# A gated sum of windowed attention and a long convolution: spectrum and products in two halves of 40 channels a group, and a new order of all tasks

## The chip, the core and the metric

The kernel runs on one core of one Trainium2 chip. The time is the device time of one launch in microseconds (us). The core's engines each run their own queue of instructions in order: TensorE (PE, matmuls and their weight loads PEld), VectorE (DVE), ScalarE (ACT), GpSimd (POOL) and SyncE (SP, which here only starts transfers).

## The reference, cut to what matters

Everything is computed for 2048 positions of 640 channels in bfloat16. `a` is attention of 32 heads over 8 earlier positions with a step of 2; `b` is a convolution of every channel with a kernel K that is itself computed from 192 complex states per channel; the two are mixed by a gate.

```python
g = _sigmoid((x * gate_w).sum(-1, keepdims=True))
a = _A_ref(x, A_wqkv, A_wo)                  # q, k, v; 8 taps; softmax; times v; times wo
P = jnp.exp(logdA[:, :, None] * l[None, None, :])
K = jnp.einsum("dn,dnl,dn->dl", Cc, P, dB).real
Kf = rfft2(pad(K)); Uf = rfft2(pad(x.T))     # length 4096
b = irfft2(Uf * Kf)[..., :L].T + x * Dskip
return g * a + (1 - g) * b
```

## The kernel before, in words

The program is a list of named tasks (`pl.add(name, engines, function, ...)`). A table of numbers, `SEQ`, sets the one order in which all 1331 tasks are written down (a letter behind a number picks the engine where there is a choice: A for ScalarE, D for VectorE; S and G pick the queue of SyncE or GpSimd for a transfer). Each engine then runs its own tasks in that order. Short-lived buffers are rings: `acq` takes a slot, `rel` gives it back; `SLOTS` has their sizes, such as two two-bank accumulators `ar` and two one-bank accumulators `tb` in PSUM.

The tasks that the change and the prediction speak of:

- **Start.** `ldx` (four loads of x), `ldt` (three of wqkv) and the parameter loads; `turn`/`tev` transpose x by TensorE and copy the result out (10 pairs, tile 128x1024, into `bufA`); `lset` blanks two tables `L` on GpSimd (three MEMSETs each).
- **Attention.** `late`/`lev` project q, k, v (accumulator `tb`); for each of eight blocks of 256 positions VectorE multiplies (`prod`, L336), TensorE sums (`lg`), the softmax follows, VectorE weighs the values (`pv`, L405), TensorE gathers (`gat`), `oT`, `wo`, `ga`, and `gaS` stores the block.
- **K by chunks.** Ten chunks (0 to 9) of 64 channels in three parts: `arg` on TensorE, `act` (sine and exponential, L778, L780) on ScalarE, `pq` on VectorE (three TENSOR_TENSOR, L797 to L799; `pq92` is the last part of the last chunk), `kmm` on TensorE, `fin`. Five ring slots let `act` run ahead of `pq`. After every five chunks `move`/`kev` lay the result out in `KE`.
- **Spectrum of K.** For each of 32 steps (16 pairs of frequencies, real and imaginary), `wl` loads 160 KB of weights, `ks` runs 20 matmuls (L917) over `KE`, and `ske` moves the 128x640 result into `sk`, on VectorE with the lag-0 term `KD` added (L926) for the real part, on VectorE or ScalarE for the imaginary one.
- **Spectrum of x.** `rows` loads; `fu`/`fue` (20 pairs) is the first stage into `Bu`; `fp`/`fe` (L1063) the second into `su`; the products `ta`, `tc`, `Y` (L1082 to L1088) multiply it with `sk` on VectorE.
- **Back.** `inv`/`cp` (20 pairs, L1112) into `C`; `yp` the last stage; `st`, `tt`, `mx` mix with `gaF`; `out` stores. SyncE starts the loads of the constants `psi` and of `gaF` (`gaf`) before that.

Before, all 32 `ks` steps come after the last chunk, since each needs the `KE` of all ten; all 20 `fu` must be done before the first `fp`; the first `inv` waits for the last products. An evacuation is one instruction:

```python
def evict(nc, en, o, i):
    if en == "A": nc.scalar.activation(o, i, ACT.Identity)
    else:         nc.vector.tensor_copy(o, i)
```

## Time and profile before

| | |
|---|---|
| time, 3 runs | 345.36 us median (344.45 to 347.49) |
| profiled execution | 345.49 us, of which the span of the core 343.7 us |
| PE | 295.3 us busy, 86%, 4630 matmuls |
| DVE | 309.3 us, 90%, 409 instructions |
| ACT | 279.3 us, 81%, 398 instructions |
| POOL | 38.2 us, 11% |
| DMA | 47.05 MB, 137 GB/s mean |
| granted TensorE clock | 0.963 mean |

A share is a mean over stages with different limits, so the stretches are looked at apart. A matmul's duration holds its way through the pipeline, so its rate is read from how far starts lie apart (in the chain of waits), not from its mean duration. "Idle before" names what an engine waited for last.

### The profile page before, as it was taken

The page shows a single profiled execution, that of the slowest core. Times are in us where ns is not written, and L with a number is a line of the kernel's source. Part 1 is how long each engine was busy: PE and PEld are TensorE (multiplying, and loading weights), DVE is VectorE, ACT ScalarE, POOL GpSimd, SP SyncE. Part 2 cuts the span into 40 slices and gives each one's busy share as a digit, 9 for nine tenths or more (in the row PEclk, how much of TensorE's full clock was granted, in tenths as well). Part 3 has the DMA queues.
Part 4 walks back from the last instruction along what each step waited for, and adds up shares of the span by engine and source line. Part 5 has one row for each costly group of instructions (what it writes and reads, how often), then busy time and mean ns, then how long its engine had stood idle before and what let it go on. Part 6 is the DMA issues. An engine that isn't in the chain of part 4 may idle for free.

```text
span 343.7 us, 10819 instructions
## 1 busy us (share of the span) xinstructions
PE 295.3 (86%) x4630; PEld 191.1 (56%) x4630; DVE 309.3 (90%) x409; ACT 279.3 (81%) x398; POOL 38.2 (11%) x61
## 2 busy tenths in 40 slices
PE   0479999999789999999999798898999999996850
PEld 0345545544344445555545354466797799976740
DVE  3898999999997999999999999979876999999890
ACT  1698999767997999999999989998566766567781
POOL 8245200064100000000000000000000000000052
PEclk9999999999958999999999989999999999998995
DMA  7994508978573116499747369822232289970046
GB/s 255 392 319 67 123 12 230 237 180 234 151 152 74 24 37 150 117 126 114 122 69 157 85 111 141 138 55 61 79 96 63 78 246 257 214 194 4 2 123 187
DMA packets 79354, 47.05 MB, mean 137 GB/s; under 512 B 49818, under 2 KB 75290, under 8 KB 79050
## 3 DMA queue, kind: packets, MB, share of 16 engines
q1 hardware_dynamic: 76298, 37.94, 50.5%
q0 software_dynamic: 2336, 7.73, 7.0%
q8 instruction: 36, 0.59, 0.8%
q10 hardware_dynamic: 672, 0.70, 0.6%
q14 instruction: 12, 0.10, 0.1%
HBM read 31.84 MB, written 14.51 MB: 135 GB/s over the span
## 4 chain that ended last, share of the span: by engine, by line
PE 52%; ACT 36%; issue 3%; DVE 3%; DMA 3%; POOL 1%; ACTq 0%; POOLq 0%; DVEq 0%
PE tb L278 13%; ACT big L778 11%; ACT big L780 8%; PE kp L917 6%; PE ar L917 6%; PE ar L764 5%; PE kps L815 4%; PE tb L411 3%; PE tb L428 3%; DMA uga<-in_A_x_dram 3%; PE ar L1063 3%; ACT bufA L1161 2%; PE ar L1031 2%; ACT C L459 2%; ACT L780 2%
## 5 line engine op out<-in xcount | busy, mean ns | idle before, releaser
L278 PE MATMUL tb<-bufA 128*128 128x512 bf16 x300 | 73.6, 388 | 1.2 <-ACT bufA L459 0.8
L778 ACT ACTIVATE big<-ar 128x720 bf16<-128x720 int16 (+1 forms) x90 | 68.2, 834 | 3.5 <-PE ar L764 2.7
L764 PE MATMUL ar<-Rarg,L 64*128 64x208 bf16 (+4 forms) x600 | 50.5, 255 | 13.1 <-ACT big L778 6.7
L278 PEld LDWEIGHTS <-bufA 128*128 128x128 bf16 x300 | 33.0, 120 | 31.8 <-issue 9.6
L780 ACT ACTIVATE big<-ar 128x832 bf16<-128x832 f32 x60 | 48.2, 887 | 0.6 <-PE ar L764 0.5
L405 DVE TENSOR_TENSOR pv<-vc,asb 128x4096 bf16<-128x4096 bf16 (+1 forms) x24 | 46.0, 1926 | 0.6 <-DMA asb<-aS 0.6
L764 PEld LDWEIGHTS <-L 64*128 64x128 bf16 x600 | 21.6, 95 | 43.4 <-issue 38.4
L1181 POOL DMA_DIRECT2D out_dram<-bufA x12 | 6.8, 571 | 240.7 <-DVE bufA L1164 240.5
L459 ACT ACTIVATE bufA<-ar 128x1024 bf16<-128x1024 f32 x25 | 25.4, 1030 | 8.1 <-PE ar L1031 6.8
L459 ACT ACTIVATE tbx<-ar 128x640 bf16<-128x640 f32 x31 | 21.6, 703 | 12.2 <-PE ar L1063 9.0
L815 PEld LDWEIGHTS <-tbx 64*64 64x64 bf16 (+1 forms) x1280 | 24.1, 113 | 7.5 <-issue 5.1
L815 PE MATMUL kps<-tbx 64*64 64x40 bf16 (+1 forms) x1280 | 27.9, 188 | 0.2 <-ACT E L459 0.2
L428 PE MATMUL tb<-wo_sb,oT 128*128 128x320 bf16 x160 | 26.4, 300 | 0.2 <-ACT ga L437 0.2
L336 DVE TENSOR_TENSOR prod<-uga 128x2048 bf16<-128x2048 bf16 x20 | 24.0, 1219 | 0.9 <-PE lg L342 0.8
L799 DVE TENSOR_TENSOR tbx<-big 128x1280 bf16<-128x1280 bf16 x30 | 24.5, 816 | 0.0
L336 DVE TENSOR_TENSOR prod<-qk 128x2048 bf16<-128x2048 bf16 x20 | 23.9, 1218 | 0.0
L459 ACT ACTIVATE uga<-tb 128x512 bf16<-128x512 f32 x28 | 16.6, 598 | 7.5 <-PE tb L278 7.3
L411 PE MATMUL tb<-pv,ind 128*64 128x512 bf16 (+1 forms) x192 | 22.6, 357 | 0.1
L797 DVE TENSOR_TENSOR tbx<-big 128x1024 bf16<-128x1024 bf16 x30 | 20.5, 683 | 2.1 <-ACT big L778 2.1
L798 DVE TENSOR_TENSOR tbx<-big 128x1024 bf16<-128x1024 bf16 x30 | 20.5, 682 | 0.0
L183 PE MATMUL ar<-ident,uga 128*128 128x128 bf16 x80 | 7.5, 255 | 14.5 <-DMA uga<-in_A_x_dram 13.4
L428 PEld LDWEIGHTS <-oT 128*128 128x128 bf16 x160 | 13.7, 97 | 8.8 <-issue 2.3
(162 smaller groups left out, 543.1 us busy)
## 6 DMA issues: line engine op xcount, KB each, us to landing
vc<-vS SPq DMA_DIRECT2D x16, 327.5 KB, 5.6
Sprm<-pc SPq DMA_DIRECT2D x12, 240.0 KB, 3.9
L<-Sprm SPq DMA_DIRECT2D x80, 36.0 KB, 2.7
xS<-bufA POOLq DMA_DIRECT2D x2, 1280.0 KB, 6.7
gaS<-ga SPq DMA_DIRECT2D x16, 160.0 KB, 2.4
uga<-xS SPq DMA_DIRECT2D x8, 320.0 KB, 6.5
uga<-gaS SPq DMA_DIRECT2D x8, 320.0 KB, 13.9
W<-c_spec SPq DMA_DIRECT2D x14, 160.0 KB, 3.0
```

The source lines that it names most:

```text
L278: nc.tensor.matmul(ppf[:], self.wq[:, which, kt, e:D:5], self.xT[:, c0 // 1024, kt, c0 % 1024:c0 % 1024 + SC], start=(kt == 0), stop=(kt = ...
L336: nc.vector.tensor_tensor(b[e][:], self.part(ch, 0)[:, e, o:o + C].unsqueeze(1).to_broadcast([128, W, C]), win(self.part(ch, 1)[:, e, :], ...
L405: nc.vector.tensor_tensor(b["pv", e][:, 0:2 * n], taps, aw, ALU.mult)
L411: nc.tensor.matmul(b["op", e][64 * a:64 * a + 64, 0:n, :], self.twin, b["pv", e][:, a:2 * n:2, w, :], start=(w == 0), stop=(w == HV - 1), ...
L428: nc.tensor.matmul(apf[:, :320], b["oT"][:, e, i * 128:(i + 1) * 128], wo_sb[:, e, hf * 320:(hf + 1) * 320], start=(e == 0), stop=(e == 4))
L459: nc.scalar.activation(o, i, ACT.Identity)
L764: nc.tensor.matmul(ar[:, g2, wd * (j - j0):wd * (k - j0)], L[rows, sb, gp, l0:l0 + 128], R[rows, c0:c0 + wd * (k - j)], start=True, stop=T ...
L778: nc.scalar.activation(dst, ar[:].bitcast(I16)[:, :, 0:2 * n:2].rearrange("p g (j n) -> p g j n", n=wd), ACT.Sin, scale=SCL)
L780: nc.scalar.activation(dst, ar[:, :, 0:n].rearrange("p g (j n) -> p g j n", n=wd), ACT.Exp)
L799: nc.vector.tensor_tensor(qq[:, :, :, :], trg[:, :, KI:].rearrange("p a (v m) -> p a v m", v=2), exq[:, :, KI:].unsqueeze(2).to_broadcast( ...
L815: nc.tensor.matmul(kps[64 * w:64 * w + 64, 2 * NM * ql:2 * NM * ql + 2 * NM], pt[rows, v, k:k + 2, :].rearrange("p a n -> p (a n)"), qq[ro ...
L917: nc.tensor.matmul(kp[64 * c:64 * c + 64, fl, 0:320], w["t"][:, fl, m, :], self.KE[:, m, c].rearrange("p g x -> p (g x)"), start=(m == 0), ...
```

## The change

The 80 channels of each of eight groups are taken in two halves of 40 (p = 0 and 1; half 0 is chunks 0 to 4). What needed all ten chunks now needs five: `ks` has 64 steps of 20 matmuls with 160 columns instead of 32 steps with 320, and every `wl` load is made for either half (64 loads). `ske` moves 128x320. `Bu` and `sk` have a half each in `bufA` and in `big`, `rows` loads by halves, `fp` of a half needs ten `fu`; one `fp` holds four frequencies of 160 columns. `ta` and `tc` are one instruction over both parts instead of two; a `Y` is two. Half 0 of `inv` uses the accumulators `ar`, half 1 `cy`, and `gaf` also waits for half 0's last products. `ks` of half 0 uses `tb`, that of half 1 `ar` and two `kp`. The `SEQ` table is new throughout (1447 tasks).

```diff
 SEQ = """
-12A 10S 13S 24 0G 11A 25 28 16S 21 29 38 22 23 26 2G 1G 7G 3G 5G 6G 99 4S 14S ...
+0G 11S 13S 12A 25 23 16G 99 7S 101S 14A 10A 6A 24 22 28 38 29 3G 4G 102 103D ...
-    SLOTS = {... "kp": 1, ... "W": 6, "su": 2}
+    SLOTS = {... "kp": 2, ... "W": 5, "W2": 3, "su": 2, "sv": 2}
...
-        for k in range(32):
+        for z in range(64):
+            p, k = divmod(z, 32)
             i, ro = divmod(k, 2)
+            tag = "W2" if p and k % 8 > 4 else "W"
...
-                            nc.tensor.matmul(kp[64 * c:64 * c + 64, fl, 0:320], w["t"][:, fl, m, :], self.KE[:, m, c].rearrange("p g x -> p (g x)"),
-                                             start=(m == 0), stop=(m == M5 - 1), ...)
+                            nc.tensor.matmul(kp[64 * c:64 * c + 64, 160 * fl:160 * fl + 160], w["t"][:, fl, m, :], self.KE[p][:, m, c].rearrange("p g x -> p (g x)"),
+                                             start=(m == 0 and fl == 0), stop=(m == M5 - 1), ...)
...
-            m = pl.add(f"ks{ro}x{i}", "P", spec, deps=[ld] + self.kevs + (ends if ro else []), ...)
+            m = pl.add(f"ks{p}{ro}x{i}", "P", spec, deps=[ld] + self.kevs[0:2 * p + 2] + (ends if p else []), ...)
...
-        self.Bu = self.bufA[:].rearrange("p (c e f q g) -> p c e f q g", c=NCH, e=2, f=32, q=8)
-        self.sk = big[:].rearrange("p (r x f) -> p r x f", r=2, f=32)
+        mem = self.bufA, big
+        self.Bu = [m[:, 0:10240].rearrange("p (c e f q g) -> p c e f q g", c=NHF, e=2, f=32, q=8) for m in mem]
+        self.sk = [m[:, 10240:].rearrange("p (r x f) -> p r x f", r=2, f=32) for m in mem]
...
                 if k == 0:
-                    for r in range(2):
-                        nc.vector.tensor_tensor(t[r], u[0], kk[r], ALU.mult)
+                    nc.vector.tensor_tensor(t, u[:, 0].unsqueeze(1).to_broadcast(one), kk, ALU.mult)
                 elif k == 1:
-                    nc.vector.tensor_tensor(u[0], u[1], kk[1], ALU.mult)
-                    nc.vector.tensor_tensor(u[1], u[1], kk[0], ALU.mult)
+                    nc.vector.tensor_tensor(u, u[:, 1].unsqueeze(1).to_broadcast(one), kk[:, ::-1], ALU.mult)
                 else:
-                    nc.vector.tensor_tensor(kk[0], t[0], u[0], ALU.subtract)
-                    nc.vector.tensor_tensor(kk[1], t[1], u[1], ALU.add)
+                    nc.vector.tensor_tensor(kk[:, 0], t[:, 0], u[:, 0], ALU.subtract)
+                    nc.vector.tensor_tensor(kk[:, 1], t[:, 1], u[:, 1], ALU.add)
...
-            np_ = 4 if fb == 7 else 1
+            np_ = 2 if p and fb == 7 else 1
...
-                prev = pl.add(f"inv{cb}{ro}", "P", inv, deps=[self.muls[fb, 0] for fb in range(7)] + [self.muls[7, cb // 5]], ...)
+                prev = pl.add(f"inv{cb}{ro}", "P", inv, deps=[self.muls[p, fb, 0] for fb in range(8 - p)] + ([self.muls[1, 7, cl // 5]] if p else []), ...)
...
-            gas.append(pl.add(f"gaf{k}", "S", gaf, deps=[self.lastfu] + gaS, after=gas[-1:]))
+            gas.append(pl.add(f"gaf{k}", "S", gaf, deps=[self.lastfu, self.muls[0, 7, 0]] + gaS, after=gas[-1:]))
```

Three places show how the new table moves instructions. Lines of the changed kernel are a few higher than those of the kernel before (L699 is L703 there, L165 is L169).

**The start.** On GpSimd, behind the first small load, the kernel before has this (`in_A_wqkv` is one `ldt`, `in_A_x` three `ldx`, `MEMSET L` one `lset`):

```order
L249 DMA ind<-c_ind 128x96
L166 DMA bufA<-in_A_wqkv_dram 128x5x640
L165 DMA uga<-in_A_x_dram 128x2560 x3
L699 MEMSET L 128x1536
L701 MEMSET L 2x1536 x2
```

The changed kernel has this on GpSimd:

```order
L247 DMA ident<-c_ident 128x128
L555 DMA ldt<-in_B_log_dt_dram 128x5
L703 MEMSET L 128x1536
L705 MEMSET L 2x1536 x2
L169 DMA uga<-in_A_x_dram 128x2560 x3
```

The three loads of x stand behind the three MEMSETs now, and the wqkv load has gone to SyncE. On VectorE the kernel before starts with eighteen parameter instructions and has no copy of a transpose; the changed one, from its third parameter instruction on, has (`CAST bufA<-ar` is a `tev`):

```order
L581 TENSOR_TENSOR wi<-cre,bim 128x960
L581 TENSOR_TENSOR wr<-cre,bre 128x960
L581 TENSOR_TENSOR wi<-wi,t_123 128x960
L465 CAST bufA<-ar 128x1024
L581 TENSOR_TENSOR wr<-wr,t_122 128x960
L465 CAST bufA<-ar 128x1024
```

So VectorE's parameter work waits for x there, and two of the first five `tev` are its own.

**The last chunk on VectorE.** Before, from `pq90` on, one after the other (`tbx<-big` is a `pq`, `bufA<-ar` a `fue`, `big<-ar,KD` the first `ske`):

```order
L797 TENSOR_TENSOR tbx<-big 128x1024
L798 TENSOR_TENSOR tbx<-big 128x1024
L799 TENSOR_TENSOR tbx<-big 128x1280
L461 CAST bufA<-ar 128x1024 x2
L439 TENSOR_SCALAR ga<-tb,g_sb 128x320
L461 CAST KE<-ar 128x2x10x40
L405 TENSOR_TENSOR pv<-vc,asb 128x4096
L926 TENSOR_TENSOR big<-ar,KD 128x320x2
```

In the changed kernel, up to the same `pq92` (`uga<-uga,bufA` is `ta` or `tc` of half 0, `bufA<-uga` its `Y`, `bufA<-tb,KD` its `ske`):

```order
L1105 TENSOR_TENSOR uga<-uga,bufA 128x1280
L935 TENSOR_TENSOR bufA<-tb,KD 128x160x2
L1107 TENSOR_TENSOR uga<-uga,bufA 128x1280
L1109 TENSOR_TENSOR bufA<-uga 128x160x4
L1110 TENSOR_TENSOR bufA<-uga 128x160x4
L409 TENSOR_TENSOR pv<-vc,asb 128x4096
L801 TENSOR_TENSOR tbx<-big 128x1024
L802 TENSOR_TENSOR tbx<-big 128x1024
L803 TENSOR_TENSOR tbx<-big 128x1280
```

Three blocks of half 0's products, and 16 `ske` of half 0 on VectorE, now stand ahead of the last part of K.

**The last loads on SyncE.** Before (`C<-c_spec` is a `wl`, `uga<-gaS` a `gaf`):

```order
L909 DMA C<-c_spec 128x640 x12
L1134 DMA uga<-gaS 32x5120 x2
L1128 DMA psi<-c_psi 128x2048
L1134 DMA uga<-gaS 32x5120 x2
L1128 DMA psi<-c_psi 128x2048
```

Changed:

```order
L1160 DMA uga<-gaS 32x5120
L1154 DMA psi<-c_psi 128x2048
L917 DMA W_1004<-c_spec 128x640
L917 DMA W_1005<-c_spec 128x640
L917 DMA tbx<-c_spec 128x640 x3
L1154 DMA psi<-c_psi 128x2048 x2
L1160 DMA uga<-gaS 32x5120 x5
```

The last weights go into ring slots (`W`, `tbx`) that must be free again, where the last twelve had places of their own in `C`; three `psi` and six `gaf` stand behind them.

279 lines of the change are left out of this document (153 added, 126 removed).

## The prediction

> **What bounds the kernel now.** The stretches first, cut at four events on VectorE: its first attention product (27.2), the first and the last part of K (94.4 and 235.8) and the first mix (326.3). The columns are length, then busy time of PE, PEld, DVE, ACT, POOL, then clock, DMA share and GB/s.
>
> ```profile
> 0.00:27.20 27.20, 11.68 (x79) 8.06 (x80) 19.84 (x29) 16.66 (x19) 14.84 (x26) 1.00 0.91 315
> 27.20:94.40 67.20, 64.15 (x504) 32.14 (x503) 65.82 (x75) 57.61 (x84) 16.55 (x24) 1.00 0.63 153
> 94.40:235.80 141.40, 130.21 (x2280) 71.96 (x2281) 135.89 (x182) 136.16 (x195) 0.00 (x0) 0.95 0.59 104
> 235.80:326.30 90.50, 84.53 (x1557) 75.17 (x1557) 78.33 (x109) 60.25 (x83) 0.00 (x0) 0.98 0.47 120
> 326.30:343.70 17.40, 4.70 (x228) 3.81 (x216) 9.45 (x19) 8.59 (x20) 6.80 (x12) 0.75 0.58 153
> ```
>
> VectorE is nearly full in three stretches: up to 326.3 it works 299.9 us and idles 26.4 (7.4, 1.4, 5.5, 12.2). In the third ScalarE is as full. In the fourth the chain of waits is TensorE's:
>
> ```profile
> 236.17 0.89 PE ar L1031 x32
> 262.51 0.79 PE tb L428 x5
> 268.68 0.66 PE ar L1063 x8
> 269.35 1.36 PE kp L917 x20
> L926 DVE TENSOR_TENSOR big<-ar,KD 128x640 bf16<-128x640 f32 x16 | 13.1, 822 | 5.7 <-PE ar L917 5.7
> 320.18 4.21 PE L1112 MATMUL cy<-GAB,big 64*128 64x128 bf16 x128 [0.30 <-DVE C L461]
> ```
>
> A `ks` step takes 1.36 us of TensorE, two `fu` 0.89, two `fp` 0.66 (0.27 each inside), a `wo` about 0.7, an `inv` 0.26; VectorE waited 5.7 us for `ks`. So the change can gain in two places: half of the `ks` leaves a stretch where TensorE is last, and half of the `inv`/`cp` leaves the serial end. It pays with work on VectorE, the fullest engine elsewhere. I therefore sum VectorE's time up to the first mix.
>
> **VectorE's work.** By form, with mean durations, and three successive rows of `pq92`:
>
> ```profile
> L461 DVE CAST E<-kps 128x320 bf16<-128x320 f32 x11 | 5.3, 480 | 0.0
> L461 DVE CAST big<-kp 128x640 bf16<-128x640 f32 x3 | 2.5, 817 | 1.0 <-PE kp L917 1.0
> L461 DVE CAST bufA<-ar 128x1024 bf16<-128x1024 f32 x5 | 6.1, 1221 | 1.6 <-PE ar L1031 1.6
> L461 DVE CAST qk<-tb 128x512 bf16<-128x512 f32 x7 | 4.8, 681 | 0.0
> L439 DVE TENSOR_SCALAR ga<-tb,g_sb 128x320 bf16<-128x320 f32 x11 | 5.9, 544 | 0.0
> L1082 DVE TENSOR_TENSOR E<-tbx,big 128x1280 bf16<-128x1280 bf16 x14 | 10.9, 817 | 0.2 <-ACT tbx L459 0.2
> 235.80 0.69 DVE L797 TENSOR_TENSOR tbx<-big 128x1024 bf16<-128x1024 bf16 x1
> 236.41 0.68 DVE L798 TENSOR_TENSOR tbx<-big 128x1024 bf16<-128x1024 bf16 x1
> 237.01 0.82 DVE L799 TENSOR_TENSOR tbx<-big 128x1280 bf16<-128x1280 bf16 x1
> ```
>
> Back to back, starts lie 0.08 us closer than durations (0.61 for 0.69), so I use duration less 0.08.
> - `ske`: 19 of 0.74 become 46 on VectorE (32 real, 14 imaginary) of 128x320. No such instruction stands in the trace; half of 0.74 is the lower bound, the 320-column cast's 0.40 the likely value, its full 0.48 the upper. 18.4 against 14.1: +4.3 (+2.9 to +8).
> - `tev` 0 to 3, `fe` 1 to 4, `lev` 14 to 19, `oT` 9 to 11: 3.4 + 2.2 + 3.0 + 1.2 = +9.8.
> - `fue` 5 to 3, `cp` 7 to 5, `fin` 11 to 5, `ga` 11 to 9, one parameter instruction less: -2.3 - 2.3 - 2.4 - 0.9 - 0.6 = -8.5.
> - The products have as many elements in 68 instructions as in 66 (a `ta` over both parts is 1280 elements, as one of its two was): about 0, and +1 because twice as many blocks have two steps each that depend on the one before and may lose the overlap of 0.08 (0 to 32 x 0.08 = 2.6).
>
> Sum +6.6, taken as +6.5 (+4 to +9). In the new order 24.9 us more stand ahead of `pq92` and 18.4 less between it and the first mix. ScalarE, counted alike, has 9 us more ahead of its last `act` and 3 us less in all.
>
> **VectorE's idle time, start.** What x waits for now:
>
> ```profile
> 3.92 1.60 POOL L165 DMA_DIRECT2D uga<-in_A_x_dram  x3
> 5.52 1.40 POOL L699 MEMSET L<- 128x1536 bf16 x1
> 6.97 2.78 POOL L701 MEMSET L<- 2x1536 bf16 x2
> 3.92 9.44 DMA uga<-in_A_x_dram
> 13.41 1.89 PE L183 MATMUL ar<-ident,uga 128*128 128x128 bf16 x16 [13.41 <-DMA uga<-in_A_x_dram]
> 20.11 4.55 PE L278 MATMUL tb<-bufA 128*128 128x512 bf16 x20 [0.75 <-ACT bufA L459]
> 5.47 1.16 DVE L577 TENSOR_TENSOR wi<-cre,bim 128x960 f32<-128x960 bf16 x1 [4.44 <-DMA bim<-in_B_B_im_dram]
> ```
>
> The MEMSETs (4.2 us) now precede the loads of x on GpSimd's queue, so the first starts at about 6.6 instead of 3.9; against that the 800 KB of wqkv are out of its queue. I put x two us later, at 15.4 (bounds: no delay, and the full 4.2). VectorE's first five parameter instructions end at 11; then it waits for `tev`: 3 us more idle than before (0 to +4.5). TensorE's first `late` (20.1 before) moves as much, since `tev` now alternate between two engines whose orders wait for each other.
>
> **Idle time, chunks.** 5.5 us before, with ScalarE as full as VectorE. With 24.9 us more for VectorE and 9 for ScalarE, ScalarE gets some 16 us ahead and no longer holds VectorE up: 3.5 (1.5 to 5.5). `pq92` then starts at 235.8 + 24.9 + 3.0 - 2.0 = 261.7.
>
> **Idle time, last stretch.** VectorE has 78.3 - 18.4 = 59.9 us from `pq92` to the first mix. TensorE, from the end of `pq92` (+2) to the last half-1 `ks`, has 41 `ks` steps of half the columns, 23 `fp`, 6 `fu`, 4 `wo`, two `gat`, and 20 `inv`. A step of 160 columns is bounded by its rate at 128 columns (`fu`: 0.89/32 = 28 ns each, so 20 are 0.56) and by no gain at all (1.36); half is 0.68, and 0.7 fits `fu` scaled to 160. 41 x 0.7 + 23 x 0.27 + 6 x 0.45 + 4 x 0.7 + 1.3 + 20 x 0.26 = 47 us, against VectorE's 50 us to its last block. The engine that waited is now the one waited for; the 12.2 us of idle go, except the 1.3 before the first mix,
>
> ```profile
> 326.26 1.93 DVE L1168 SCALAR_TENSOR_TENSOR bufA<-cy,om,uga 128x320 bf16<-128x320 f32 x4 [1.27 <-PE cy L1154]
> 316.64 8.34 DVE L461 CAST C<-cy 128x1024 bf16<-128x1024 f32 x7
> ```
>
> and some for two nearly full engines with two-slot accumulators between them: 3.0 (1.3 to 12.2). The serial end shrinks inside this: before, VectorE copied seven `cp` in 8.3 us after its last product, now four.
>
> **The sum.** First mix at 261.7 + 59.9 + 3.0 = 324.6 instead of 326.3; the 17.4 us behind it keep their tasks: span 342.0. The profiled execution took 345.49 against a span of 343.7, and the median of the runs is 345.36, so 1.8 is added: **343.8 us**, 0.5% less than before. What the pipeline gains in idle time, VectorE largely pays back in work and in a later start.
>
> **Rivals.**
> - *The pipelining wins outright.* x lands as early as before (-3), `ske` cost their lower bound (-1.5), the last stretch idles 1.3 (-1.7): 337.6. For it: TensorE, ScalarE and DMA all have room in the last stretch. Against it: VectorE's fullest stretch above is 98% full, and this asks for about as much over three stretches.
> - *The idle time stays.* In the last stretch TensorE (47) and VectorE (50) are both nearly full, coupled through two `ar`, two `kp` and two `tb`, and each waits for the other's turn: idle remains 12.2 and the time is 343.8 + 9.2 = 353. It is slower than before once that idle passes 4.6, by over 1% once it passes 8. For it: the evacuation of every smaller step has its own wait. Against it: ScalarE and VectorE, just as coupled, lost only 5.5 us in 141.
> - *The last constants come too late.* The last weights can only be loaded when a slot is free, about 12 us of VectorE's work ahead of its last block, and three `psi` and six `gaf` queue behind them.
>
> ```profile
> 285.00:308.00 23.00, 22.78 (x330) 21.96 (x327) 21.33 (x29) 13.84 (x22) 0.00 (x0) 1.00 0.97 229
> psi<-c_psi SPq DMA_DIRECT2D x4, 512.0 KB, 13.0
> uga<-gaS SPq DMA_DIRECT2D x8, 320.0 KB, 13.9
> ```
>
>   Four `psi`, eight `gaf` and the last weights filled the DMA (0.97) for 23 us; the three and six are 3.5 of 4.6 MB, about 17 us, against 20 until `yp` needs them (those 12, and 8 for the last block and four `cp`). If they take 23 us, the end moves by 3: 347.
> - *Weight loads show.* Each load of 128x64 weights now serves 160 columns instead of 320. If the 20 loads set the rate, a step keeps its 1.36 us; 41 steps cost 0.66 x 41 = 27 us more, TensorE's 3 us of slack hide little, and the time is 368. The `fu` row speaks against it: the same load before only 128 columns, at 28 ns. The Trainium skill, "TensorE: Matmul & The Clock Gate", section "LDWEIGHTS (loading the stationary operand)", puts a load at columns/1.2 ns, which is 53 ns for 64 columns; by that rule, with loads one after another, a step would be an estimated 1.07 us and the sum 355. The `fu` row contradicts that for two column tiles side by side.
>
> **How the numbers follow.** Chances: the forecast, with the late constants as a variant, 0.50; the win 0.27; idle time stays 0.19; weight loads 0.04. About 1% is what a measurement of this kernel can tell from no change. Of the forecast's 0.50, 0.08 reaches below 341.9, and 0.03 lies above 348.8; the slower cases are 0.19 and 0.04, of which 0.05 end short of 348.8. Faster 0.35, same 0.44, slower 0.21. The range is 335.5 to 352: below, the win with the chunks' idle at its bound (337.6 - 2.0); above, idle in the last stretch kept to all but 1 us. The forecast's own range is 339 to 348.
>
> **What would show it.** VectorE's busy total about 316 (309.3 before); its idle before 27 to 33 us grown by some 3, with a copy of a transpose waiting for x; `ske` near 0.48 us in duration; `pq92` at about 262; 20 matmuls of a `ks` in 0.7 us; less than 6 us idle on VectorE in the last stretch, and the first mix near 325. I am wrong if `pq92` starts before 255, if `ks` steps stay near 1 us, or if `yp` waits for `psi`.

## The result: 6.7% slower, and where the profile after shows the time

The changed kernel takes 368.66 us in the median of four runs (367.59 to 372.60), the kernel before, on the same chip, 346.23 (344.45 to 347.49): 1.067 times as long, 95% interval 1.058 to 1.077. Ratios, here and below, leave out executions that took over 1.5% longer than the fastest of the same kernel. The forecast was 343.8 us with a range of 335.5 to 352. The profiled execution took 367.59 us, its span is 365.8.

The same five stretches as in the prediction, cut at the same events on VectorE (first attention product, first and last part of K, first mix); the columns are length, busy time of PE, PEld, DVE, ACT, POOL, then clock, DMA share and GB/s:

```profile
0.00:35.20 35.20, 14.96 (x93) 9.64 (x94) 23.05 (x29) 16.94 (x20) 15.41 (x27) 1.00 0.69 245
35.20:105.60 70.40, 68.25 (x507) 34.36 (x506) 68.55 (x84) 53.79 (x76) 13.46 (x19) 1.00 0.65 158
105.60:271.50 165.90, 150.85 (x2982) 95.39 (x2983) 155.98 (x208) 155.68 (x224) 0.00 (x0) 0.99 0.56 112
271.50:348.80 77.30, 63.98 (x1608) 55.38 (x1608) 60.17 (x103) 43.32 (x65) 0.00 (x0) 0.98 0.58 156
348.80:365.80 17.00, 6.02 (x231) 5.51 (x219) 9.54 (x19) 8.59 (x20) 6.73 (x12) 0.70 0.61 157
```

Length less VectorE's busy time is VectorE's idle time. With it the whole difference up to the first mix can be laid beside the forecast (us; "start" is the first row, "attention" the second, "chunks" the third):

| VectorE | before | forecast | after |
|---|---|---|---|
| work up to the first mix | 299.9 | 306.4 | 307.8 |
| idle, start | 7.4 | 10.4 | 12.2 |
| idle, attention | 1.4 | 1.4 | 1.9 |
| idle, chunks | 5.5 | 3.5 | 9.9 |
| idle, last stretch | 12.2 | 3.0 | 17.1 |
| first mix | 326.3 | 324.6 | 348.8 |

Work was forecast to 1.4 us. Idle time was to fall from 26.4 to 18.3 and rose to 41.1. The first mix came 24.2 us later than forecast: 14.1 of them are idle time of the last stretch, 6.4 of the chunks, 2.3 of the first two stretches, and 1.4 are work. The last stretch did become 13.2 us shorter, but `pq92` moved back by 35.7.

Its pieces came out as forecast. Two groups of VectorE's instructions and one row of TensorE's timeline (start, length; the 40 matmuls are two `ks` steps in 1.58 us, the last one's way through the pipeline, some 0.2, included):

```profile
L935 DVE TENSOR_TENSOR bufA<-tb,KD 128x320 bf16<-128x320 f32 x16 | 7.7, 486 | 1.9 <-PE tb L926 1.6
L935 DVE TENSOR_TENSOR big<-ar,KD 128x320 bf16<-128x320 f32 x16 | 7.5, 486 | 6.2 <-PE ar L926 6.2
284.43 1.58 PE L926 MATMUL tb<-KE,W 128*64 128x160 bf16 x40
```

A `ske` of 128x320 costs 0.486 us (forecast 0.48), a step of 160 columns 0.7 us (forecast 0.7): half of the old 1.36, so weight loads do not show.

VectorE's waits in the chunks (waited for; us, times, longest), first in the kernel before, then in the changed one:

```profile
DVE tbx L797 <- ACT big L778: 2.1, 2, 1.2
DVE uga L461 <- PE tb L278: 1.8, 2, 1.6
DVE prod L336 <- PE lg L342: 0.8, 2, 0.6
...
DVE oT L465 <- PE tb L415: 2.0, 3, 1.0
DVE bufA L935 <- PE tb L926: 1.6, 3, 1.0
DVE prod L340 <- PE lg L346: 1.6, 2, 1.4
DVE bufA L465 <- PE tb L926: 1.5, 2, 1.3
DVE bufA L465 <- PE ar L1039: 1.3, 1, 1.3
DVE tbx L801 <- ACT big L784: 0.2, 1, 0.2
```

With the shorter ones, not shown, VectorE waited 2.1 us for ScalarE and 2.9 for TensorE before, and 0.2 and 8.6 after. So the wait for ScalarE did go, and a larger one for TensorE came. 5.3 us of it are for results in `tb` (2.1 before), the two accumulators that half 0's `ks` now share with the attention tasks; TensorE itself waits 3.2 us there for a free `tb`, before 0.2.

VectorE's waits in the last stretch (waited for; us, times, longest), then ScalarE's timeline at its end:

```profile
DVE C L465 <- PE cy L1136: 6.3, 2, 5.1
DVE big L935 <- PE ar L926: 6.2, 8, 2.3
DVE bufA L1194 <- PE cy L1180: 2.0, 1, 2.0
...
329.82 1.94 ACT L463 ACTIVATE C<-ar 128x1024 bf16<-128x1024 f32 x2 [2.69 <-PE ar L1136]
332.14 0.46 ACT L463 ACTIVATE big<-kp 128x320 bf16<-128x320 f32 x1 [0.39 <-PE kp L926]
332.50 1.92 ACT L463 ACTIVATE C<-ar 128x1024 bf16<-128x1024 f32 x2
335.13 3.77 ACT L463 ACTIVATE C<-ar 128x1024 bf16<-128x1024 f32 x4 [0.71 <-PE ar L1136]
342.48 5.61 ACT L463 ACTIVATE C<-cy 128x1024 bf16<-128x1024 f32 x6 [3.57 <-issue]
```

The wait for `ks` results is what it was (6.2 us; 5.7 before), for half as many columns. And half 0's inverse is not out of the way when the products end: eight of its ten `cp` (`C<-ar`) run one behind the other on ScalarE from 329.8 to 338.9, through two `ar` slots, with half 1's own behind them (`C<-cy`: six there on ScalarE, four on VectorE). Half 0's last product had ended at 298.0; but its first `inv` ran at 311.8, and only 72 of its 160 matmuls before the last `ks` ended at 332.1. In that time TensorE waited 0.5 us at them, so it is mainly their place in the order that made them late, and not a lack of slots. VectorE's last product ends at 335.8; from there to the first mix it is 13.0 us, 8.3 of them waits for `cy`. Before, it was 9.7 us (316.6 to 326.3).

### The profile page after: what moved, and what is told of

Same layout as the page of the kernel before. It is cut to its first block, busy times and chain, and to the rows that moved or that the text cites. A ratio compares the mean times of both kernels' runs of the same rounds, so it can differ in the third digit from the quotient of the medians.

```text
span 365.8 us, 12449 instructions
## 1 busy us (share of the span) xinstructions
PE 304.1 (83%) x5398; PEld 200.3 (55%) x5398; DVE 317.3 (87%) x439; ACT 278.3 (76%) x402; POOL 35.6 (10%) x58
## 5 line engine op out<-in xcount | busy, mean ns | idle before, releaser
L768 PE MATMUL ar<-Rarg,L 64*128 64x208 bf16 (+4 forms) x600 | 49.2, 250 | 12.3 <-ACT big L782 6.6
L784 ACT ACTIVATE big<-ar 128x832 bf16<-128x832 f32 x60 | 49.1, 899 | 2.7 <-PE ar L768 2.4
L282 PEld LDWEIGHTS <-bufA 128*128 128x128 bf16 x300 | 33.9, 120 | 30.9 <-issue 7.7
L926 PEld LDWEIGHTS <-W 128*64 128x64 bf16 x1040 | 38.1, 111 | 6.1 <-issue 2.9
L1207 POOL DMA_DIRECT2D out_dram<-bufA x10 | 5.6, 568 | 259.6 <-ACT big L1187 257.0
L926 PE MATMUL tb<-KE,W 128*64 128x160 bf16 x640 | 27.7, 237 | 0.9 <-ACT ga L441 0.5
L187 PE MATMUL ar<-ident,uga 128*128 128x128 bf16 x80 | 8.5, 272 | 20.2 <-DMA uga<-in_A_x_dram 15.7
L803 DVE TENSOR_TENSOR tbx<-big 128x1280 bf16<-128x1280 bf16 x30 | 24.5, 817 | 0.0
L415 PE MATMUL tb<-pv,ind 128*64 128x512 bf16 (+1 forms) x192 | 21.8, 347 | 0.2
L801 DVE TENSOR_TENSOR tbx<-big 128x1024 bf16<-128x1024 bf16 x30 | 20.5, 683 | 0.7 <-issue 0.5
L463 ACT ACTIVATE tbx<-ar 128x640 bf16<-128x640 f32 (+1 forms) x15 | 10.4, 716 | 13.6 <-PE ar L1086 12.0
L802 DVE TENSOR_TENSOR tbx<-big 128x1024 bf16<-128x1024 bf16 x30 | 20.5, 683 | 0.0
```

The costliest lines, as they stand in the source:

```text
L282: nc.tensor.matmul(ppf[:], self.wq[:, which, kt, e:D:5], self.xT[:, c0 // 1024, kt, c0 % 1024:c0 % 1024 + SC], start=(kt == 0), stop=(kt = ...
L415: nc.tensor.matmul(b["op", e][64 * a:64 * a + 64, 0:n, :], self.twin, b["pv", e][:, a:2 * n:2, w, :], start=(w == 0), stop=(w == HV - 1), ...
L768: nc.tensor.matmul(ar[:, g2, wd * (j - j0):wd * (k - j0)], L[rows, sb, gp, l0:l0 + 128], R[rows, c0:c0 + wd * (k - j)], start=True, stop=T ...
L784: nc.scalar.activation(dst, ar[:, :, 0:n].rearrange("p g (j n) -> p g j n", n=wd), ACT.Exp)
L803: nc.vector.tensor_tensor(qq[:, :, :, :], trg[:, :, KI:].rearrange("p a (v m) -> p a v m", v=2), exq[:, :, KI:].unsqueeze(2).to_broadcast( ...
L926: nc.tensor.matmul(kp[64 * c:64 * c + 64, 160 * fl:160 * fl + 160], w["t"][:, fl, m, :], self.KE[p][:, m, c].rearrange("p g x -> p (g x)") ...
```

## Experiments

The change has two parts that can be had apart: the halves, and the new order of all tasks. That comes first, then single suspects, then the load of each engine, then the order by stretches. All times are medians of four runs beside runs of the kernel before on the same chip (its medians were 345.0 to 347.4); a ratio is to that kernel.

### The halves and the order, apart

**Halves without the order.**

```diff
-                for m in range(M5):
+                for p in range(2):
+                    for m in range(M5):
...
-    nc.tensor.matmul(kp[..., fl, 0:320], w["t"][:, fl, m, :], self.KE[:, m, c] ...
+    nc.tensor.matmul(kp[..., fl, 160 * p:160 * p + 160] ..., w["t"][:, fl, m, :], self.KE[:, m, c, :, 40 * p:40 * p + 40], ...
```

> The kernel before in its own order, with each step of the spectrum done as two groups of 20 products of 160 columns from the same weights (each weight tile is loaded into TensorE twice), and each eviction as two of 128x320. The products behind it and the DMAs are as before. Theory (halving itself is cheap, the order costs): VectorE has 19 evictions of 0.82 us as two of 0.486 us, +2.9 us, ScalarE 13 of them; TensorE's steps stay near 1.5 us: 347 to 352 us. Rival (twice the loads of weights into TensorE is what costs): the step takes 2.2 us or more, and 32 of them on the path of the last stretch bring 360 to 370 us.

354.82 us (351.21 to 355.73), ratio 1.021 (1.015 to 1.028): 8.6 us more than the kernel before, between theory and rival. Only `ks` and `ske` are halved here (the cut shows `ks`); the weights are loaded once, and the tasks around them are whole. The chain of waits shows what is in it (start, us, what):

```profile
298.82 1.43 PE kp L918 x40
300.24 0.27 PE ar L1065 x4
300.52 0.73 PE ar L918 x21
301.25 3.32 issue
304.57 1.49 PE ar L918 x19
```

A step of 40 matmuls with 160 columns takes 1.38 to 1.43 us, as 20 with 320 did. But in the step that follows, TensorE stops after 21 matmuls for 3.3 us, and the profile names nothing that it waited for ("issue"). Three such stops (3.3, 1.5 and 0.8) add up to 5.6 us. They lie between 294 and 312 us, where the tail's constants, whose loads start from 287.8 to 298.2, fill the transfer engines.

**The same with the constants later.**

```diff
             def gaf(e, k=k):
+                if k == 0:
+                    queue(nc, e).dma_start(self.tick[:], self.sk[0:1, 1, 0:8, 28])
```

> The run with halves in the old order again, but the 4.7 MB of the tail's constants (`gaf`, `psi`) start only when `ske1x14` has evicted: a DMA of 16 bytes that reads its result stands ahead of them on SP's queue. In the first such run TensorE stopped inside single steps (3.3 us in `ks0x13`, 1.5 in `ks1x11`, 0.8 in `ks1x14`) while these loads filled the transfer engines, each time just ahead of or at a 16 KB packet of its instruction queue. Theory (with 40 products to a step TensorE reads its instructions faster than they come through the filled transfer engines): the pauses go, and what is left of +8.6 us is the +2.9 of the evictions: 348 to 351.5 us. Rival (the pauses have another cause, or the constants now come too late): 353 to 358 us.

351.97 us (350.72 to 353.26), ratio 1.018 (1.013 to 1.023). The steps now run through without a stop, and the last `ske` of the real parts starts at 307.7 instead of 315.6 (before: 306.9). The stop has not gone, though; it went where the constants went, into the inverse products:

```profile
320.86 2.14 PE L1114 MATMUL cy<-GAB,big 64*128 64x128 bf16 x69 [0.24 <-DVE C L461]
327.44 1.82 PE L1114 MATMUL cy<-GAB,big 64*128 64x128 bf16 x34 [4.44 <-issue]
```

So stops follow the burst of transfers. If every us of a stop is a us of the end, the two runs stand at some 349 and 348 without them, and halved `ks` and `ske` by themselves cost an estimated 2 to 3 us, near the 2.9 us of the evictions.

**The order without the halves.** The kernel before, with the common tasks up to `kmm921` in the new order:

```diff
 SEQ = """
-12A 10S 13S 24 0G 11A 25 28 16S 21 29 38 22 23 26 2G 1G 7G 3G 5G 6G 99 4S 14S ...
+0G 11S 13S 12A 25 23 16G 99 7S 101S 14A 10A 6A 24 22 28 38 29 3G 4G 102 103D ...
```

> The kernel before (whole steps of 320 columns, one load of each weight, all of its spectrum behind `kmm921`), but all that both kernels have in common stands, up to `kmm921`, in the changed kernel's order and on the changed kernel's engines; behind `kmm921` it keeps its own order. So it is the new order without the halves, as the run before this was the halves without the new order. Theory (the new order of the head and the chunks is what costs, since VectorE and ScalarE wait more in it): `pq92` comes at about 258 to 262, as in the run with half 0 deferred, the last stretch loses some 11 us of evictions that were moved ahead, and the time is 357 to 364 us. Rival (the new order costs nothing by itself, it is the half steps in it that get in each other's way): 344 to 350 us.

366.58 us (365.73 to 367.14), ratio 1.057 (1.051 to 1.063), a little above what the theory gave. `pq92` came where the theory had it, at 260.1; but the last stretch got 2.5 us shorter, where the theory moved some 11 us of work out of it. The stretches:

```profile
0.00:34.50 34.50, 13.78 (x92) 9.50 (x94) 23.15 (x30) 16.98 (x20) 15.43 (x27) 1.00 0.67 239
34.50:104.80 70.30, 67.56 (x496) 34.34 (x503) 68.45 (x84) 53.73 (x76) 14.06 (x21) 1.00 0.67 163
104.80:260.10 155.30, 134.98 (x2412) 78.89 (x2419) 141.23 (x179) 146.59 (x209) 0.00 (x0) 0.95 0.51 89
260.10:348.10 88.00, 79.35 (x1402) 69.15 (x1403) 68.35 (x101) 55.33 (x77) 0.00 (x0) 0.96 0.47 123
```

VectorE works 301.2 us up to the first mix, 1.3 more than before, and idles 46.9 (11.4, 1.9, 14.1, 19.7), 20.5 more. **The new order up to `kmm921`, without the halves, costs 20 us; with them the change costs 22.** These are two differences and not shares of one sum, because this mixture has waits of its own, one in the chunks and one in the last stretch:

```profile
DVE bufA L462 <- PE ar L1032: 5.9, 1, 5.9
DVE KE L462 <- PE ar L890: 4.0, 1, 4.0
```

Neither the kernel before nor the changed one has a single wait near that length at these places, so part of the 20 us may come from an order without the pieces that it was made for. Against this kernel the changed one has 6.6 us more work and 5.9 less idle time (41.1): its halves move `pq92` out by 11.4 and shorten the last stretch by 10.7, and the sum is nearly nothing. In the last stretch here TensorE is busy 79 of 88 us; the 10 us of VectorE's work that went ahead (78.3 before, 68.4 now) shortened it by 2.5.

**The order, the halves, and nothing early.** The changed kernel with half 0 behind `kmm921`:

```diff
-... 824 395A 968 969 825 ... 851 423A 971 515 ... 518 424 972D 982 985 402 ...
+... 824 395A 825 ... 851 423A 515 ... 518 424 402 ...
```

> The changed kernel with all steps, evictions and products of half 0 (and their weights from the sixth on) moved behind `kmm921`, the last product of the chunks; nothing else changes place. Theory (the pieces of half 0 gain nothing among the chunks, since VectorE is the engine that works through in either place, and its idle time comes from the chain of TensorE and evictions in whichever stretch they stand): `pq92` falls from 271.5 to 245 or 250, the last stretch grows by as much, 366 to 373 us. First rival (the early pieces themselves hold up the chunks and cost what was lost): 350 to 358 us. Second rival (the early pieces do gain, and without them TensorE bounds the last stretch): over 376 us.

384.24 us (383.57 to 384.49), ratio 1.108 (1.103 to 1.113): the second rival. The chunks and the last stretch:

```profile
104.80:260.60 155.80, 135.07 (x2415) 78.94 (x2420) 141.27 (x179) 146.67 (x210) 0.00 (x0) 0.95 0.50 97
260.60:366.10 105.50, 86.86 (x2165) 75.72 (x2167) 75.89 (x131) 52.83 (x80) 0.00 (x0) 0.97 0.54 148
```

Half 0 moves `pq92` out by 10.9 us where its pieces stand among the chunks, and lengthens the last stretch by 28.2 where they stand behind. So in this order the early pieces gain 15.6 us. The idea of the halves works; it pays back what two half passes, one behind the other, cost in the last stretch, and no more.

### Single suspects

**The loads of x ahead of `lset1`.**

```diff
-0G 11S 13S 12A 25 23 16G 99 7S ... 1159G 100G 18G ...
+0G 11S 13S 12A 25 23 16G 7S ... 1159G 100G 18G 99 ...
```

> The changed kernel with one thing moved: `lset1`, GpSimd's row of MEMSETs (4.1 us), stands behind the loads of x on GpSimd's queue, not ahead of them. Theory (the late x starts VectorE late, and nothing behind it takes the delay up): VectorE's first eviction `tev0` comes some 4 us earlier, its idle time ahead of `late0` falls from 12.2 us to about 8, `late0` starts at 20 instead of 24.3, and all behind it keeps that: 363 to 365 us. Rival (the delay is taken up later, by waits for TensorE and ScalarE in the chunks): `late0` is earlier but `pq92` and the end are not: 367 to 369 us.

367.41 us (365.79 to 368.41), ratio 1.059 (1.054 to 1.064): the rival. `tev0` starts 2.2 us earlier (14.7), yet `prod00` only 0.5 (34.7), and `pq92` not at all (272.0). TensorE's timeline shows how it was lost; first this kernel's, then the changed one's, 25 matmuls of the same kind each, and this kernel's window from 28 to 32 us:

```profile
28.50 0.97 PE L188 MATMUL ar<-ident,uga 128*128 128x128 bf16 x8 [2.13 <-DVE bufA L466]
29.26 6.91 PE L283 MATMUL tb<-bufA 128*128 128x512 bf16 x25
28.00:32.00 4.00, 3.50 (x15) 1.79 (x15) 2.82 (x5) 2.67 (x5) 0.00 (x0) 0.57 0.00 0
```
```profile
30.70 0.61 PE L187 MATMUL ar<-ident,uga 128*128 128x128 bf16 x8 [1.79 <-DVE bufA L465]
31.16 5.56 PE L282 MATMUL tb<-bufA 128*128 128x512 bf16 x25
```

TensorE gets there 2 us sooner, waits 2.1 us for an eviction, and then runs at a granted clock of 0.57 from 28 to 32 us: 0.28 us a matmul instead of 0.22. The changed kernel, behind a pause of 1.8 us at the same place, keeps a clock of 1.00. The Trainium skill, "TensorE: Matmul & The Clock Gate", section "What's actually happening", has TensorE at half clock again after an idle window of about 3.4 us; here the clock fell behind a pause of 2.1 us.

**The last weights ahead of `gaf` and `psi`** (all twelve loads behind `wl131` on SP's queue):

```diff
-... 1129 1394 1132 ... 1141 1395 1142 1143 1390 1144 ... 1318 1156 1157 ...
+... 1129 1132 ... 1141 1142 1143 1144 ... 1318 1156 1394 1395 1390 1391 ...
```

> The changed kernel with one thing moved: all loads of `gaf` and `psi` stand behind the last load of weights, `wl131`, on SP's queue. Theory (late weights hold up the last steps of half 1: `gaf0` waits on SP for the landing of `gaS7` with `wl123` behind it, and the tail's constants then share the transfer engines with the weights): the waits of the steps 10x11 to 10x15 for their weights, some 4 us, go, `Y171` ends at about 331 to 332 instead of 335.8, and the time is 363 to 365 us. Rival (these waits are covered, since the serial end is set by the evictions `cp` on ScalarE, or `psi` and `gaf` are now what is late): 367 to 371 us.

368.05 us (367.46 to 369.85), ratio 1.063 (1.057 to 1.069): the rival. From 311 to 332 us the steps no longer wait for weights (0.8 us in the changed kernel), `Y171` ends at 335.2 instead of 335.8, and the rest is as it was: the steps wait longer for `ar` slots instead (1.3 us there, in the changed kernel 0.9).

**Eight evictions of the head back on ScalarE.**

```diff
-... 167D ... 138D ... 144D ... 142D ... 146D ... 180D ... 171D ... 163D ...
+... 167A ... 138A ... 144A ... 142A ... 146A ... 180A ... 171A ... 163A ...
```

> The changed kernel, with eight evictions of 128x512 (`lev6`, 8, 9, 10, 18, 20, 22, 26) in the head put back from VectorE to ScalarE, where the kernel before had them, at the same places of the order. VectorE loses 8 x 0.68 = 5.4 us of work ahead of the chunks, ScalarE, which idles 17.6 of the 68.8 us between `late0` and `arg0s00`, gains 8 x 0.6 = 4.8. Theory (VectorE's work bounds the head, it idles 2.5 us there): the chunks start 4 to 5 us earlier and the end follows: 363 to 365 us. Rival (the chunks do not start by VectorE, or ScalarE's load in the chunks takes the gain): 367 to 369 us.

372.07 us (371.57 to 377.42), ratio 1.073 (1.067 to 1.079). Neither the theory nor the rival: it is not faster, with 5.4 us less for the engine that I had held to be the bound. That it is slower than the changed kernel the two ratios do not show; their intervals overlap. In the profiled execution (377.4 us) the first `act` comes at 100.3 instead of 95.1, and VectorE waits 7.0 us for ScalarE in the first 105 us, for results of the parameters' operations above all, where the changed kernel has no wait for ScalarE of 0.3 us or more. In this execution, then, ScalarE's idle time in the head was not free time: what it does there is waited for.

**Half 0's inverse behind half 1's steps.**

```diff
-... 1302A 1115 1330 1123 ... 1124 1125 1331 1332A 1127 ... 1150 1153 1333 1145 ...
+... 1302A 1115 1123 ... 1124 1125 1127 ... 1150 1153 1145 ...
```

> The changed kernel; the inverse products `inv00` to `inv91` of half 0 stand behind the last step of half 1, `ks11x15`, and their evictions `cp0` to `cp9` behind `Y171`, by turns on ScalarE and VectorE. Theory (in the last stretch the inverse products hold one of the two `ar` slots, so that half 1's steps and its `fp` go through the other alone): `ks11x15` ends at 326 to 329 instead of 332.1 and `Y171` at 329 to 332 instead of 335.8, then ten more evictions on two engines take some 5.5 us where 3.1 stood: 363 to 368 us in all. Rival (half 1's steps are held up by their weights and by VectorE's products): `Y171` stays at 335 to 336, and the end is 2 to 4 us later, 370 to 373 us.

374.56 us (369.12 to 375.76), ratio 1.073 (1.060 to 1.087): inside the changed kernel's interval, so the run does not tell which of the two is faster. In the profiled execution (374.7 us) the last step ends at 330.9, 1.2 us sooner, and `Y171` at 336.6, 0.8 us later, nearer to the rival; the first mix comes 19.4 us behind that instead of 13.0. But TensorE stops there, ahead of the late `inv`, for 3.7 us (331.3 to 335.0) with no wait named, as in the runs with halves, so how much of the 19.4 us the ten late evictions cost is not shown.

### The load of each engine in the chunks

Each of these takes work from one engine there, 5 to 6 us as forecast, and leaves the order as it is. Their kernels leave out part of the copies, of the products or of the steps' matmuls.

```diff
-                evict(nc, en, self.Bu[p][:, cl, c2], b["bp"][:].rearrange(...))
+                w = 8 if en == "A" and not p else 32
+                evict(nc, en, self.Bu[p][:, cl, c2][:, 0:w], b["bp"][:].rearrange(...)[:, 0:w])
```

> The changed kernel; of the ten evictions `fue0` to `fue9` the nine on ScalarE copy a quarter of their columns, so ScalarE has some 5.9 us less to do in the chunks (9 x about 0.65 us) and VectorE as much as ever. ScalarE and VectorE are each busy 94% of the chunks. Theory A (both bind there, each delay of the one is handed to the other): the time falls by 2 to 4 us, 364.5 to 366.5. Theory V (VectorE alone bounds the chunks, as the prediction's sum had it): by less than 1, 367.5 to 369. Theory S (ScalarE alone does): by 5 to 6, 362 to 364.

```diff
-                x = slice(160 // np_ * z, 160 // np_ * (z + 1))
+                x = slice(160 // np_ * z, 160 // np_ * (z + 1)) if p or fb > 2 else slice(0, 40)
```

> The changed kernel; the products `ta`, `tc` and `Y` of half 0's first three groups work on a quarter of their columns, so VectorE has some 5.2 us less to do in the chunks (9 operations, about 0.57 us each) and ScalarE as much as ever. Theory A (both bind): the time falls by 2 to 4 us, 364.5 to 366.5. Theory V (VectorE alone): by 4.5 to 5.5, 363 to 364. Theory S (ScalarE alone): by less than 1, 367.5 to 369.

```diff
-                for m in range(M5):
+                n5 = M5 if p or i > 10 else 3
+                for m in range(n5):
```

> The changed kernel; the steps of half 0 up to the eleventh pair do three of their five sets of products, so TensorE has 22 x 8 products of 34 ns = 6.1 us less to do in the chunks, and each step's result is out 0.28 us sooner; VectorE and ScalarE have as much to do as ever. Theory T (TensorE and what waits for it sets the chunks' length, since 5 us less on VectorE or on ScalarE changed nothing): `pq92` and the end come 4 to 6 us earlier, 362 to 364.5 us. Rival (no engine's work sets it, the order does, in which each engine waits for the others in turn): 366.5 to 369 us.

ScalarE less: 368.43 us (1.065; 1.058 to 1.071). VectorE less: 369.39 (1.066; 1.061 to 1.072). TensorE less: 365.70 (1.057; 1.050 to 1.064), 3 us less than the changed kernel, between theory and rival, with intervals of the ratios that overlap. The chunks of the three, in this order:

```profile
105.40:271.90 166.50, 151.50 (x2975) 95.51 (x2983) 156.13 (x208) 150.75 (x224) 0.00 (x0) 0.98 0.55 112
106.60:271.70 165.10, 150.15 (x2947) 94.85 (x2955) 151.90 (x208) 154.44 (x222) 0.00 (x0) 0.98 0.57 112
104.70:270.90 166.20, 148.85 (x2801) 90.71 (x2809) 155.96 (x208) 155.93 (x224) 0.00 (x0) 0.97 0.55 112
```

ScalarE is busy 4.9 us less in the first, VectorE 4.1 in the second, TensorE 2.0 in the third (181 matmuls fewer; the row counts matmuls that overlap once), and the stretch stays at 165 to 167 us: what an engine has less to do, it waits more. In all three it is TensorE that VectorE waits for, 8.4, 11.8 and 7.8 us by the list of waits (8.6 in the changed kernel), and yet TensorE's work by itself does not set the length either. Theory A fails with V and S. All three engines are some 90% busy or more, each waits for the others in turn, and a little room on one is no room. That is also the price of filling them: against the kernel before, the chunks of the changed one hold 20.1 us more for VectorE, 19.5 for ScalarE and 20.6 for TensorE, and are 24.5 us longer.

### The order by stretches

**The new head alone, in the kernel before** (`SEQ` up to `arg0s00` as in the order without the halves, the rest as before):

```diff
 SEQ = """
-12A 10S 13S 24 0G 11A 25 28 16S 21 29 38 22 23 26 2G 1G 7G 3G 5G 6G 99 4S 14S ...
+0G 11S 13S 12A 25 23 16G 99 7S 101S 14A 10A 6A 24 22 28 38 29 3G 4G 102 103D ...
```

> The kernel before (whole steps); only the tasks that both kernels issue ahead of `arg0s00` stand in the changed kernel's order and on its engines, the rest as before. Theory (the order's loss adds up by stretches: 11 us of the 20 in the head): the first `act` at 93 to 96 us instead of 83, the chunks and the last stretch as long as before, 355 to 359 us. Rival (the late head is taken up behind, since the chunks have their own pace): 346 to 350 us.

357.53 us (353.93 to 358.99), ratio 1.032 (1.025 to 1.040). The theory: the first `act` starts at 94.1 instead of 83.3, and nothing behind takes it up.

```profile
0.00:36.00 36.00, 16.36 (x93) 9.96 (x94) 23.02 (x29) 17.44 (x20) 15.43 (x27) 0.95 0.66 232
36.00:109.20 73.20, 66.29 (x491) 32.58 (x490) 69.51 (x82) 53.90 (x76) 12.04 (x22) 0.95 0.58 146
109.20:249.20 140.00, 129.09 (x2279) 72.27 (x2279) 135.80 (x182) 135.54 (x194) 0.00 (x0) 0.96 0.55 104
249.20:339.70 90.50, 85.56 (x1553) 76.35 (x1553) 78.33 (x108) 60.34 (x83) 0.00 (x0) 0.96 0.46 120
```

The first mix comes 13.4 us later than before: 6.8 are VectorE's work (306.7 instead of 299.9, evictions taken over from ScalarE that the chunks of the kernel before do not give back), 6.6 are idle time, 5.6 of them in the start. The chunks (140.0, before 141.4) and the last stretch (90.5) are those of the kernel before.

**Its two parts.** First the changed kernel with the old order up to `prod00`, then the kernel before with the new one behind `prod00`:

```diff
-0G 11S 13S 12A 25 23 16G 99 7S 101S 14A 10A 6A 24 22 28 38 29 3G 4G ...
+12A 10S 13S 24 0G 11A 25 28 16S 21 29 38 22 23 26 2G 1G 7G 3G 5G 6G 99 ...
```

> The changed kernel; the tasks that the kernel before issues up to its first `prod00` (loads, parameters, the turning of x, the first projections) stand in that kernel's order and on its engines, the rest of the head, the chunks and the last stretch in the changed kernel's. Theory (some 8 of the 11 us that the head loses are lost ahead of `prod00`, where the evictions of x, `tev`, stand between the parameters' operations on VectorE and ScalarE, and the rest of the program moves with the head): `prod00` at 28 to 30 us instead of 35, the first `act` at 86 to 90 instead of 95, 358 to 363 us. Rival (what is gained there is lost behind, as with `lset1`): 365 to 369 us.

```diff
-... 124 260 141 112 142A 137 122G 547G 138A 139 140A ...
+... 124 260 101S 112 113D 119A 116 98 122S 80 81 166 167D 137 138D 143 114 144D 131 139 ...
```

> The kernel before; the head up to `prod00` stands in its own order, the rest of the head, from `prod00` to `arg0s00`, in the changed kernel's, and all behind in its own. With the whole head in the changed kernel's order it took 357.5 us. Theory (the cost lies ahead of `prod00`): 346 to 351 us, the first `act` at 84 to 88. Rival (it lies behind `prod00`, where VectorE has the evictions that stood on ScalarE): 354 to 358 us.

366.14 us (365.07 to 366.45; 1.059, 1.053 to 1.066) and 355.22 (354.51 to 356.58; 1.029, 1.023 to 1.034). Both times the rival: with the old start `prod00` comes at 28.9, 6.3 us earlier than in the changed kernel, and the first `act` only 2.8 earlier (92.3); in the other run `prod00` is at 29.1 and the first `act` at 92.7, against 27.2 and 83.3 before. The start's gain does not outlive the attention part, which is paced by its own order.

**Splices that failed.** Four runs put one stretch of one kernel's order beside the other's. The changed kernel with the old head up to `arg0s00`:

```diff
-0G 11S 13S 12A 25 23 16G 99 7S 101S ...
+12A 10S 13S 24 0G 11A 25 28 16S 21 ...
```

> The changed kernel, in which the tasks that both kernels have in common and that the changed one issues ahead of `arg0s00`, the first product of the chunks, stand in the order and on the engines of the kernel before; from `arg0s00` on all is as in the changed kernel. Theory (the new order of the head costs what the head shows, and the chunks start that much earlier without it): the first `act` comes at 83 to 86 instead of 95 us, the chunks and the last stretch keep their lengths, 356 to 360 us. Rival (the chunks' length depends on what stands behind in them and takes the gain up, as it did with `lset1`): 365 to 369 us.

The kernel before with the new chunks behind its own head:

```diff
-... 187 276 295 70 ... 193A 87 190 191A 172 ... 252G 279A 280 368 345 215 ...
+... 187 276 70 ... 193A 87 172 ... 252G 279A 345 215 ...
```

> The kernel before (whole steps) with its own head; the common tasks between `arg0s00` and `kmm921` stand in the changed kernel's order and on its engines. Theory (9 us of the 20 are lost here: ScalarE, busy 147 of 152.5 us in these chunks, gets 9 us of `fue` from the last stretch, where it idles 30 of 90): chunks of 163 to 167 us, `pq92` at 247 to 251, the last stretch 88, 353 to 358 us. Rival (the loss is all in the head): 345 to 350 us.

The order without the halves, with nine pairs back at their old places (16 places in the table):

```diff
-... 493 933 1084A 467D 525 1085 934 918 ... 526 471D 935 1086A 936 920 ...
+... 493 933 467D 525 1085 918 ... 526 471D 920 472 921A 473A 494 495A ...
```

> The run with the new order alone again, but the first stage of the transform of x, `fu5` to `fu13` with `fue5` to `fue13`, stands behind `kmm921` again, as in the kernel before; some 8 us of ScalarE's evictions leave the chunks. Theory (the new order puts work into chunks in which ScalarE is full, and takes it from a stretch in which ScalarE idles): `pq92` falls from 260 to 251 or 253, the last stretch grows by 0 to 3 us, 358 to 362 us. Rival (the chunks' length does not go by ScalarE's load, as when `fue0` to `fue9` were cut in the changed kernel): `pq92` at 257 to 260 and 366 to 370 us.

The changed kernel with the common tasks in their old order, head and chunks alike (257 places):

```diff
-0G 11S 13S 12A 25 23 16G 99 7S 101S ...
+12A 10S 13S 24 0G 11A 25 28 16S 21 ...
```

> The changed kernel, in which all that both kernels have in common stands in the order and on the engines of the kernel before, in the head, the chunks and behind; the steps and evictions of half 0 that the changed kernel has among the chunks stay at the same `act` and `pq` as there, 22 steps, and the products of half 0 come as soon as `fu9` is out, behind `pq92`. Theory (the order of the common tasks is what costs, the halves gain where they stand early): `pq92` comes at 244 to 250 us, between the 236 of the kernel before and that with 11 to 15 us of half 0 added, the last stretch at 85 to 92, and the time is 346 to 355 us. Rival (the chunks of the kernel before are so full, ScalarE 96%, that the early steps push them out by more than they save): 356 to 366 us.

They took 373.54 (1.076; 1.067 to 1.084), 371.87 (1.077; 1.069 to 1.084), 386.54 (1.117; 1.112 to 1.123) and 410.53 us (1.182; 1.171 to 1.193): slower than theory and rival alike. In each, waits that neither kernel has drown what was to be measured; VectorE's longest one in each but the last, in this order:

```profile
85.14 0.69 DVE L465 CAST uga<-tb 128x512 bf16<-128x512 f32 x1 [6.88 <-PE tb L282]
100.55 0.69 DVE L462 CAST uga<-tb 128x512 bf16<-128x512 f32 x1 [15.00 <-PE tb L279]
265.22 0.69 DVE L798 TENSOR_TENSOR tbx<-big 128x1024 bf16<-128x1024 bf16 x1 [9.80 <-ACT big L779]
```

In the third nine pairs of tasks moved back, and what hangs on them with them; `pq90` then waits 9.8 us for its `act`. In the last VectorE waits for the half steps, and these for their slots (TensorE waits 13.6 us for a free `tb` at them); VectorE's waits there (us, times, longest):

```profile
DVE bufA L936 <- PE tb L927: 21.4, 8, 7.1
```

So these runs do not tell how the 8.6 us of idle time that the chunks gain in the new order, and the 7.5 that the last stretch gains, come about. The list of waits of that run names what is waited for (in the chunks 5.9 us for the one `fu` and 5.3 for `gat`, in the last stretch 10.7 for `ks` and 4.0 for the layout of K), not why it is late. That stays open. They do show how much an order can cost with the same tasks.

## Why the prediction was wrong, point by point

- **VectorE's work: right.** +6.5 forecast, +7.9 measured; `ske` and the `ks` step came out to 2%, and the weight loads did not show.
- **Start: mechanism right, size off.** Idle time +3.0 forecast, +4.8 measured. The wait that was named is there: VectorE waits 6.2 us for the first `tev`. With x loaded ahead of `lset1` it still waits 3.9, so 2.3 us are the late x, and the rest is a `tev` that stands so early in VectorE's order.
- **Chunks: wrong.** The step that failed is "ScalarE gets some 16 us ahead and no longer holds VectorE up", as a reason for less idle time. Its second half came true: VectorE's waits for ScalarE fell from 2.1 to 0.2 us. But the 5.5 us of before were in part waits for TensorE (2.9), and the forecast put nothing at TensorE's side of this stretch, where half 0's steps, its `fp` and more `fu` were to run; these waits rose to 8.6, and idle time came to 9.9 instead of 3.5. The lead was wrong as well: ScalarE had 11.4 us more to do up to its last `act`, where I had 9, it idled in the attention part (16.6 us, before 9.6), and it reached its last `act` 6.6 us ahead of `pq92` (0.8 before). Why TensorE's results came late there is open: work taken from any one engine left the stretch as long as it was.
- **Last stretch: wrong, and the largest term.** The step that failed is "the engine that waited is now the one waited for; the 12.2 us of idle go". It compared two totals, 47 us of TensorE and 50 of VectorE, and set the idle time to what the smaller one leaves over. VectorE idled 17.1 us, and it still waited for TensorE: 6.2 us for `ks`, 8.3 for the inverse. TensorE took 58.5 us from the end of `pq92` (273.6) to the end of the last `ks` (332.1), with only 9 of the 20 `inv` done in that time; by the sum's own prices that is some 44 us of work. 7.0 us of the 58.5 are idle, 4.5 of them for what VectorE or ScalarE had to free or finish and 2.1 for weights.
- **The serial end: wrong, inside the last stretch.** It was to shrink by three `cp`. It grew from 9.7 to 13.0 us, because four of half 0's ten evictions and half 1's whole inverse still stood there. The forecast took it for done that half 0's inverse is out of the way by then; in the order of the table it is not.
- **The rivals.** "The idle time stays" named the right wait, with a chance of 0.19: in the last stretch each of two engines waits for the other. Its price of 353 was still 16 us short, since idle time there did not stay but grew by 5, and since it took the order for free in the other stretches, as the forecast did. The constants and the weight loads were not it.
- **The signs.** None of the three that were to show an error came (`pq92` before 255, `ks` near 1 us, `yp` waiting for `psi`): they watched the prices of single pieces, which were right. The one that caught it is the idle time of the last stretch, 17.1 us where less than 6 was to show.
- **What was never priced is the order itself.** Every idle term started from the kernel before and was changed by an argument on loads. The experiments give the order +20 us without the halves; halved `ks` and `ske` in the old order +6 to +9 with TensorE's stops and an estimated 2 to 3 without; both together +22. The cleanest piece is the new head in the kernel before: +12 us, with all stretches behind it as long as before.

No run was faster than the kernel before. The best with a part of the change, the halves in the old order with later constants, is 1.8% slower (1.3 to 2.3%).

## What to carry to other kernels

Where three engines are each 90% busy and hand each other small buffers, neither the fullest engine's sum nor its old idle time says what a new order costs. Split the old idle time by the engine that it waits for, and ask of each what the change gives that engine to do; price a reordering as a cost of its own, and separate it from the change that it serves, in the forecast and on the chip (one kernel with the old pieces in the new order, one with the new pieces in the old). Work that is moved ahead must land in a stretch that has room on every engine it touches; moved into a full one, it comes back as length: beside the same order without the halves, half 0's pieces moved `pq92` out by 11.4 us and shortened the last stretch by 10.7. And time that one task is given earlier counts only if the engine's next wait is not for something else: most of the small corrections here gave nothing.
